# The last 64 rows of the contraction in an mLSTM and bilinear kernel: half-array pairs of matmuls against full-array matmuls on a stacked tile

## The chip, the cores and the metric

The kernel runs on one core of a Trainium2 chip. The metric is the device time of one execution in microseconds. A core has a tensor engine (PE; its weight loads are listed apart as PEld), a vector engine (DVE), a scalar engine (ACT), GpSimd (POOL) and a queue engine (SP) that issues all DMAs of this kernel in the order in which they stand on it.

## The reference

```python
# per batch b and head h, over 768 steps t (B=4, H=8, D=40)
m_new = maximum(f[t] + m, i[t])
C = exp(f[t] + m - m_new) * C + exp(i[t] - m_new) * outer(v[t], k[t])
n = exp(f[t] + m - m_new) * n + exp(i[t] - m_new) * k[t]
y[t] = sigmoid(o[t]) * (C @ q[t]) / maximum(abs(n . q[t]), 1)
# then over all 3072 tokens, x = y with its 8 heads of 40 side by side: 320 columns
a = x @ w_a              # 320 x 1536
b = x @ w_b              # 320 x 1536
out = (a * b) @ w_out    # 1536 x 320
```

The weights come as float64. The bilinear layer contracts over 320 rows of x: two full tiles of 128 rows and a last one of 64. That last one is what the change is about.

## The kernel before

**Attention.** The 768 steps of each of the four sequences are cut into chunks of 128 tokens, 24 chunks in all, and `chunks` lists them by step and sequence. A chunk goes through stages named by letters: decay weights (E), splits and transposes of q and k (A), scores (B), values (C), the denominator and the gated output y (F), the state's update (U), and last `stage_d`, which turns y to x. y lies in the tile `osig`, tokens on the partitions and 320 columns in the free dimension. `stage_d` transposes it into one PSUM tile `pX` of 3 x 128 columns and evicts it in two parts: a rounded high part (`xh`, float32r) and the rest (`xl`).

**The last 64 columns of y.** `stage_d` writes them twice: a transpose puts them into rows 0 to 63 of the third part of pX (L596), and an ordinary matmul with the identity puts the same columns into rows 64 to 127 (L597). Rows 0 to 63 of `xh[:, 2]` become the high part. For rows 64 to 127 ACT copies the high part into a tile of its own, `xd` (L602), and DVE writes the low part into `xh[64:, 2]` (L606). The third part of xh so holds high above low.

**Bilinear layer.** The chunks are grouped into nine token blocks of `sizes = [2, 2, 3, 3, 3, 3, 3, 2, 3]` chunks, so a matmul of the layer streams 256 or 384 columns. `moe_block` walks over the 12 hidden tiles `ff` of 128 columns. For each, `up` accumulates w_a's product in `acc[0]` and w_b's in `acc[1]` (PSUM tiles `pu`, three buffers). An exact product is built from three terms (high times high, high times low, low times high) for each of the first two row tiles: six matmuls on the full 128 x 128 array (L694). For the last 64 rows a seventh one takes `wh[j][:, 2]`, in which the high part of the weights stands in both halves, times `xh[:, 2]`. The low weights of these rows are in a tile `wt`, those of w_a in rows 0 to 63 and those of w_b in rows 64 to 127, and two matmuls of 64 rows (L702) multiply them: `wt[0:64]` times `xh[0:64, 2]` into acc[0], and `wt[64:]` times `xd[64:]` into acc[1]. ACT (or DVE) copies acc[0] to `g`, DVE multiplies acc[1] by it, splits the product, and `down` (L664) multiplies it by w_out into `pd`, two hidden tiles later.

**Weights.** `weights` turns the float64 words into float32r parts in 32 stages, eight for each group of 384 columns, spread over roughly the first 135 us. The fifth stage of a group is that of the last 64 rows: ACT rounds the high parts (L338), two DMAs on SP's queue copy each of them into the other half of `wh[j][:, 2]` (L341), and the low parts go to `wt`, by POOL in the first two groups and by PE and an ACT copy in the last two (L360).

**Order.** Pieces of attention are mixed into the matmuls of a token block at a fixed rate (the last loop of the program), and a scheduler then sets the order on each engine before the kernel runs; on the chip each engine follows that order.

Of the kernel before, what the change touches and what calls it, by code (L numbers as in the profile page):

```python
# [20 lines left out]
def kernel(  # L21
# [37 lines left out]
    wh = [wpool.tile([P, 3, DFF], F32R, name=f"wh{j}") for j in range(2)]  # L59
    wl = [wpool.tile([P, 2, DFF], F32R, name=f"wl{j}") for j in range(2)]  # L60
    wt = wpool.tile([P, DFF], F32R, name="wt")
# [11 lines left out]
    # words on their way to the weights, in the room of q's and k's parts till then  # L73
# [8 lines left out]
    # constants and parts of the first chunks' exponents, in the last state's room till then  # L82
# [14 lines left out]
    # columns of log inputs, state weights and the next chunk's decays, chunk by chunk  # L97
# [8 lines left out]
    sizes = [2, 2, 3, 3, 3, 3, 3, 2, 3]       # chunks of a token block  # L106
# [41 lines left out]
    def load_o(c):  # L148
        """Output gates of a chunk of every sequence."""
        osig[c] = apool.tile([P, B, DM], F32, tag="osig", name=f"osig{c}", bufs=1)  # L150
        for b in range(B):
            nc.sync.dma_start(
                osig[c][:, b].rearrange("t (h d) -> t h d", h=H),
                o_gate[b, :, c * P:(c + 1) * P, :].rearrange("h t d -> t h d"),
            )
        hot[0] = 3
        nc.scalar.activation(osig[c], osig[c], AF.Sigmoid)
# [22 lines left out]
        # the first chunks' log decays and inputs, and their parts as bfloat16  # L180
# [21 lines left out]
        # the later chunks  # L202
# [51 lines left out]
    def weight_stages():  # L254
        for ch in range(DFF // WCH):
            cols = slice(ch * WCH, (ch + 1) * WCH)
            for kt in range(2):
                for j, w in ((0, w_a), (1, w_b)):
# [11 lines left out]
                cols,  # L270
# [9 lines left out]
    def need(x):  # L280
        """Weight stages before x are emitted."""
        while ready[0] < x:
            next(conv)

    def weights():
# [46 lines left out]
        def second(x):  # L332
# [3 lines left out]
            kept = [(rows, h, l) for rows, h, l in hl if l is not None]  # L336
            for rows, h, l in kept:
                nc.scalar.copy(h, W[rows])  # L338
            if len(hl) == 4:
                for j in range(2):  # L340
                    nc.sync.dma_start(  # L341
                        hl[j * 3 + (1 - 2 * j)][1].bitcast(F32), hl[3 * j][1].bitcast(F32)
                    )
            if x < 2 * STAGES and x % STAGES < 6 or x < 2 * STAGES:
                for rows, h, l in kept:
                    nc.gpsimd.tensor_tensor(W[rows], W[rows], h.bitcast(F32), op=ALU.subtract)
                (nc.gpsimd if x < 2 * STAGES and x % STAGES < 6 else nc.vector).tensor_tensor(low(x), W, r, op=ALU.add)
                return
            pc = ps_up.tile([P, NTB], F32, tag="pu", name=f"pc{x}")[:, :n]
            if x % STAGES < (4 if x < 2 * STAGES else STAGES):  # L350
                for rows, h, l in kept:
                    nc.gpsimd.tensor_tensor(l, W[rows], h.bitcast(F32), op=ALU.subtract)
                nc.tensor.matmul(pc, eye[0], low(x), start=True, stop=False)
                nc.tensor.matmul(pc, eye[0], r, start=False, stop=True)
            else:
                nc.tensor.matmul(pc, ident, W, start=True, stop=False)
                nc.tensor.matmul(pc, eye[0], r, start=False, stop=False)
                for rows, h, l in kept:
                    nc.tensor.matmul(pc[rows], eye[1][rows, rows], h, start=False, stop=True)
            nc.scalar.copy(low(x), pc)  # L360
# [21 lines left out]
    def stage_e(n):  # L382
        """Decay weights of a chunk, masked to s <= t."""
# [14 lines left out]
    def stage_a(n):  # L398
        """Exact three-part bfloat16 splits of q, k and v; q and k transposed on the way."""
# [6 lines left out]
        # parts of a head's row: q as (h, h, m) and (h, m, l), k as (m, h, h) and (l, m, h)  # L406
# [152 lines left out]
    def stage_f(n):  # L559
# [14 lines left out]
        yv = y.rearrange("p (h d) -> p h d", h=H)  # L574
# [7 lines left out]
    def stage_d(n):  # L582
# [3 lines left out]
        if t0 == 0:  # L586
            xt[k_] = (
                mpool.tile([P, 3, NTB], F32R, tag="xh", name=f"xh{k_}", bufs=2),
                mpool.tile([P, 2, NTB], F32R, tag="xl", name=f"xl{k_}", bufs=2),
                mpool.tile([P, NTB], F32R, tag="xd", name=f"xd{k_}", bufs=2),  # L590
            )
        xh, xl, xd = xt[k_]
        pX = ps_at.tile([P, 512], F32, tag="pat", name=f"pX{n}")
        for t in range(2):
# [346 lines left out]
```

## Time and profile before

| what | value |
|---|---|
| time, median of 3 runs | 642.67 us (635.86 to 645.09) |
| span of the profiled execution, first to last instruction | 641.1 us |
| PE busy (matmuls) | 604.1 us, 94%, 4926 matmuls |
| DVE busy | 478.1 us, 75% |
| ACT busy | 240.8 us, 38% |
| POOL busy | 206.5 us, 32% |
| mean granted clock of the tensor engine | 0.944 |

The profile gives no other time of its own execution than its span, which is 1.6 us below the median of the timed runs. A matmul's duration in the trace covers its whole way through the array, and matmuls overlap; what one costs is the distance from its start to the start of the next. A row of the timeline has the start and the duration in us, the engine, the line, the operation, what it writes and reads, and the tile. Rows that follow each other with the same text are merged (x2).

### The profile page before, as it was taken

The numbers are of one execution on the slowest core, as the hardware profiler recorded it, in microseconds if no ns is written. First come the engines' busy times: TensorE is split into PE (matmuls) and PEld (weight loads), VectorE is DVE, ScalarE is ACT, GpSimd is POOL, SyncE is SP. The second block draws the span as 40 slices with busy tenths as digits, with TensorE's granted clock in tenths as the row PEclk, the third lists the DMA queues.
The fourth block names the chain that finished last, engine by engine and source line by source line (L and its number), as shares of the span: only waits on it lengthen the run. The fifth ranks groups of instructions, "written<-read, shape, count | busy, mean of one in ns | idle before, by whom it ended". The sixth has DMA issues, their size and how long they took to land. (4 is left out here: it accounts for less than half of the span.)

```text
span 641.1 us, 12928 instructions
## 1 busy us (share of the span) xinstructions
PE 604.1 (94%) x4926; PEld 525.6 (82%) x4926; DVE 478.1 (75%) x1012; ACT 240.8 (38%) x562; POOL 206.5 (32%) x230
## 2 busy tenths in 40 slices
PE   4766998999999999999999999989999999999997
PEld 3554887888878888888888888878898899888896
DVE  6999899875785979689686889589949674843332
ACT  5645456564332353233433244343414512310011
POOL 2778665654440343044213233213303301100000
PEclk9655988698999999999999999989999999999999
DMA  9565656464445486347943645637635903300000
GB/s 195 97 164 129 149 131 155 140 133 89 118 101 85 107 153 147 77 122 138 172 83 97 136 100 117 162 88 117 137 83 121 170 11 91 52 1 22 0 1 32
DMA packets 196339, 67.66 MB, mean 106 GB/s; under 512 B 178452, under 2 KB 189556, under 8 KB 196276
## 3 DMA queue, kind: packets, MB, share of 16 engines
q1 hardware_dynamic: 196276, 66.83, 48.2%
q8 instruction: 39, 0.64, 0.4%
q14 instruction: 24, 0.20, 0.1%
HBM read 41.18 MB, written 5.97 MB: 74 GB/s over the span
## 5 line engine op out<-in xcount | busy, mean ns | idle before, releaser
L694 PE MATMUL pu<-xh,wh 128*128 128x384 f32 (+1 forms) x648 | 219.3, 344 | 1.3 <-ACT xh L601 1.3
L694 PE MATMUL pu<-xl,wh 128*128 128x384 f32 (+1 forms) x432 | 142.1, 329 | 0.4 <-DVE xl L603 0.4
L694 PE MATMUL pu<-xh,wl 128*128 128x384 f32 (+1 forms) x432 | 141.0, 326 | 0.0
L694 PEld LDWEIGHTS pu<-xh,wh 128*128 128x128 f32 x648 | 124.6, 194 | 19.9 <-issue 13.6
L709 DVE TENSOR_TENSOR g<-pu,g 128x384 f32<-128x384 f32 (+1 forms) x108 | 55.0, 509 | 97.6 <-PE pu L694 57.3
L708 ACT COPY g<-pu 128x384 f32<-128x384 f32 (+1 forms) x90 | 39.7, 442 | 141.9 <-PE pu L702 129.1
L664 PE MATMUL pd<-woh,gh 128*128 128x320 f32 x288 | 92.4, 323 | 0.0
L664 PE MATMUL pd<-wol,gh 128*128 128x320 f32 x288 | 89.6, 313 | 0.0
L664 PE MATMUL pd<-woh,gl 128*128 128x320 f32 x288 | 86.4, 316 | 0.0
L694 PEld LDWEIGHTS pu<-xl,wh 128*128 128x128 f32 x432 | 84.0, 194 | 1.7 <-DVE xl L603 0.6
L694 PEld LDWEIGHTS pu<-xh,wl 128*128 128x128 f32 x432 | 83.8, 194 | 0.7 <-issue 0.7
L491 POOL TENSOR_TENSOR vw<-va,gtab 128x336 f32<-128x336 f32 x14 | 11.3, 805 | 175.5 <-PE pU L525 153.3
L664 PEld LDWEIGHTS pd<-woh,gh 128*128 128x128 f32 x288 | 54.8, 190 | 4.4 <-issue 2.9
L394 ACT ACTIVATE gbc<-gbc,gtab 128x128 f32<-128x128 f32 x160 | 49.1, 389 | 16.6 <-POOL gbc L387 16.4
L664 PEld LDWEIGHTS pd<-wol,gh 128*128 128x128 f32 x288 | 54.9, 190 | 0.5 <-issue 0.5
L664 PEld LDWEIGHTS pd<-woh,gl 128*128 128x128 f32 x288 | 53.4, 190 | 0.5 <-issue 0.3
L713 DVE TENSOR_TENSOR gl<-g,gh 128x384 fp32r<-128x384 f32 (+1 forms) x92 | 50.7, 551 | 1.8
L711 DVE CAST gh<-g 128x384 fp32r<-128x384 f32 (+1 forms) x108 | 45.8, 424 | 1.7
L702 PE MATMUL pu<-xh,wt 64*128 64x384 f32 (+1 forms) x108 | 46.2, 428 | 0.0
L702 PE MATMUL pu<-xd,wt 64*128 64x384 f32 (+1 forms) x108 | 46.2, 427 | 0.0
L575 POOL TENSOR_TENSOR osig<-osig,den 128x320 f32<-128x320 f32 x24 | 19.5, 814 | 68.4 <-DVE den L570 50.7
L387 POOL TENSOR_SCALAR_AFFINE_SELECT gbc<-gbc 128x1024 f32<-128x1024 f32 x20 | 25.6, 1279 | 43.0 <-DMA va<-in_v_dram 32.4
(153 smaller groups left out, 1173.8 us busy)
## 6 DMA issues: line engine op xcount, KB each, us to landing
gbc<-g_dram SPq DMA_DIRECT2D x20, 512.0 KB
va<-in_v_dram SPq DMA_DIRECT2D x24, 160.0 KB
qk<-in_q_dram SPq DMA_DIRECT2D x24, 160.0 KB
qk<-in_k_dram SPq DMA_DIRECT2D x24, 160.0 KB
osig<-in_o_gate_dram SPq DMA_DIRECT2D x24, 160.0 KB
raw<-in_moe_w_out_dram SPq DMA_DIRECT2D x12, 320.0 KB
out_dram<-o SPq DMA_DIRECT2D x24, 160.0 KB
raw<-in_moe_w_a_dram SPq DMA_DIRECT2D x8, 384.0 KB
```

What stands on the lines that cost most here:

```text
L387: nc.gpsimd.affine_select(E, E, pattern=[[0, H], [1, P]], compare_op=ALU.is_ge, fill=-1e30, base=0, channel_multiplier=-1,)
L394: nc.scalar.activation(E[:, h], E[:, h], AF.Exp, bias=beta[:, h:h + 1])
L491: nc.gpsimd.tensor_tensor(vw, nat(n)[1], w_col(c, b).unsqueeze(2).broadcast_to([P, H, DV]), op=ALU.mult)
L575: after["p"] = [nc.gpsimd.tensor_tensor(yv, yv, den.unsqueeze(2).broadcast_to([P, H, D]), op=ALU.mult).ins]
L664: nc.tensor.matmul(pd[t][:, 0:DM], a[:, cols], w[:, ff, :], start=(ff == 0 and first), stop=(ff == NF - 1 and last),)
L694: nc.tensor.matmul(acc[j], a, r, start=(j == 0 and x == 0), stop=(j == 1 and x == len(terms) - 1),)
L702: nc.tensor.matmul(acc[h], wt[h * 64:h * 64 + 64, cols], r, start=(h == 1), stop=(h == 0))
L708: (nc.vector.tensor_copy if ff in [1, 2] else nc.scalar.copy)(g, acc[0])
L709: nc.vector.tensor_tensor(g, acc[1], g, op=ALU.mult)
L711: nc.vector.tensor_copy(gh, g)
L713: (nc.gpsimd if kb * 12 + ff < 16 else nc.vector).tensor_tensor(gl, g, gh.bitcast(F32), op=ALU.subtract)
```

## The change

The last 64 rows no longer use half-array matmuls.

- y gets 64 more columns: `osig` is 384 wide for each sequence, and after DVE has written y, ACT copies its last 64 columns behind it (one new instruction for each chunk, in `stage_f`).
- `stage_d` makes three full 128 x 128 transposes. The third yields the last 64 columns in both halves. One ACT copy writes xh and one DVE subtraction writes xl, both 3 x 128 wide. The tile `xd`, its ACT copy and the second DVE subtraction are gone.
- The weights of the last 64 rows are stacked: `wh[0][:, 2]` holds w_a's high part in rows 0 to 63 and its low part in rows 64 to 127, `wh[1][:, 2]` the other way round. The low parts are made in a staging tile `ct` with one buffer and reach their half by two DMAs on SP's queue, issued after the low parts are made (before, the DMAs carried the high parts and were issued after those). `wt` is gone.
- In `up` each accumulator takes eight full-array matmuls: the stacked tile times `xh[:, 2]` and times `xl[:, 2]` in place of the seventh matmul and the pair. The count stays 16 for each hidden tile.

```diff
     def load_o(c):
-        osig[c] = apool.tile([P, B, DM], F32, tag="osig", name=f"osig{c}", bufs=1)
+        osig[c] = apool.tile([P, B, 3 * P], F32, tag="osig", name=f"osig{c}", bufs=1)
...
                 [
-                    (slice(j * 64, j * 64 + 64), wh[j][u * 64:u * 64 + 64, 2, cols],
-                     wt[j * 64:j * 64 + 64, cols] if u == j else None)
-                    for j in range(2) for u in range(2)
+                    (slice(j * 64, j * 64 + 64), wh[j][j * 64:j * 64 + 64, 2, cols],
+                     wh[j][64 - j * 64:128 - j * 64, 2, cols])
+                    for j in range(2)
                 ],
...
         def low(x):
-            hl = stages[x][1]
-            return hl[0][2] if len(hl) == 1 else wt[:, stages[x][2]]
+            hl = stages[x][1]
+            if len(hl) == 1:
+                return hl[0][2]
+            return cpool.tile([P, WCH], F32R, tag="ct", name="ct", bufs=1)
+
+        def cross(x, lo):
+            hl = stages[x][1]
+            if len(hl) > 1:
+                for rows, h, l in hl:
+                    nc.sync.dma_start(l.bitcast(F32), lo[rows].bitcast(F32))
...
-            if len(hl) == 4:
-                for j in range(2):
-                    nc.sync.dma_start(
-                        hl[j * 3 + (1 - 2 * j)][1].bitcast(F32), hl[3 * j][1].bitcast(F32)
-                    )
...
-            nc.scalar.copy(low(x), pc)
+            nc.scalar.copy(lo, pc)
+            cross(x, lo)
...
         nc.vector.tensor_tensor(yv, num[:, :, 0:D], yv, op=ALU.mult)
+        nc.scalar.copy(y[:, DM:], y[:, 2 * P:DM])
...
-        for t in range(2):
+        for t in range(3):
             nc.tensor.transpose(pX[:, t * P:(t + 1) * P], s["y"][:, t * P:(t + 1) * P], ident)
-        nc.tensor.transpose(pX[0:64, 2 * P:3 * P], s["y"][:, 2 * P:], ident)
-        nc.tensor.matmul(pX[64:, 2 * P:3 * P], s["y"][:, 2 * P:], ident, start=True, stop=True)
...
         after["a"] = [nc.scalar.copy(xh[:, :, cols], px).ins]
-        nc.scalar.copy(xd[64:, cols], px[64:, 2])
         nc.vector.tensor_tensor(
-            xl[:, :, cols], px[:, 0:2], xh[:, 0:2, cols].bitcast(F32), op=ALU.subtract
-        )
-        nc.vector.tensor_tensor(
-            xh[64:, 2, cols], px[64:, 2], xd[64:, cols].bitcast(F32), op=ALU.subtract
+            xl[:, :, cols], px, xh[:, :, cols].bitcast(F32), op=ALU.subtract
         )
...
-                    (wh[j][:, 2, cols], xh[:, 2, :]),
+                    (wh[j][:, 2, cols], xh[:, 2, :]), (wh[j][:, 2, cols], xl[:, 2, :]),
                 ]
                 for x, (a, r) in enumerate(terms):
                     nc.tensor.matmul(
-                        acc[j], a, r, start=(j == 0 and x == 0),
-                        stop=(j == 1 and x == len(terms) - 1),
+                        acc[j], a, r, start=(x == 0), stop=(x == len(terms) - 1),
                     )
                     yield
-                if j == 0:
-                    for h, r in enumerate((xh[0:64, 2, :], xd[64:, :])):
-                        nc.tensor.matmul(
-                            acc[h], wt[h * 64:h * 64 + 64, cols], r, start=(h == 1), stop=(h == 0)
-                        )
-                        yield
```

The scheduler sets the order anew. On PE, in hidden tile 8 of the eighth token block (two chunks), this stood before around the two half-array matmuls (`pu_8_0` is acc[0], `pu_8_1` is acc[1], wh_72 and wh_73 are w_a's and w_b's high parts, pd is the output of `down`):

```order
L694 MATMUL pu_8_0_7524<-xl_6400,wh_72 128x256
L694 MATMUL pu_8_0_7524<-xh_6399,wl_74 128x256
L694 MATMUL pu_8_0_7524<-xh_6399,wh_72 128x256
L702 MATMUL pu_8_0_7524<-xh_6399,wt 128x256
L664 MATMUL pd_0_6921<-woh,gh_6_7483 128x320
L664 MATMUL pd_0_6921<-wol,gh_6_7483 128x320
L702 MATMUL pu_8_1_7525<-xd_6401,wt 128x256
L694 MATMUL pu_8_1_7525<-xh_6399,wh_73 128x256
L694 MATMUL pu_8_1_7525<-xl_6400,wh_73 128x256
```

And at the same place now:

```order
L693 MATMUL pu_8_0_7470<-xl_6359,wh_72 128x256
L693 MATMUL pu_8_0_7470<-xh_6358,wl_74 128x256
L693 MATMUL pu_8_0_7470<-xh_6358,wh_72 128x256
L693 MATMUL pu_8_0_7470<-xl_6359,wh_72 128x256
L662 MATMUL pd_0_6874<-woh,gh_6_7429 128x320
L662 MATMUL pd_0_6874<-wol,gh_6_7429 128x320
L693 MATMUL pu_8_1_7471<-xh_6358,wh_73 128x256
L693 MATMUL pu_8_1_7471<-xl_6359,wh_73 128x256
```

The two half-array matmuls, here apart with two matmuls of `down` between them, are gone; the eighth term of acc[0] stands in the place of the first. In the whole order before, 85 of the 108 pairs stand next to each other and 23 are apart; of the 36 pairs of two-chunk blocks 20 are together and 16 apart, of the 72 of three-chunk blocks 65 and 7.

On PE, `stage_d` of a chunk in the middle of the program stood before like this (pX is its PSUM tile, osig the tile of y, and a row with x2 is two instructions):

```order
L595 MATMUL pX_4734<-ident,osig_3792 128x128 x2
L596 MATMUL pX_4734<-ident,osig_3792 64x128
L597 MATMUL pX_4734<-ident,osig_3792 64x128
L694 MATMUL pu_7_0_5014<-xh_3543,wl_74 128x384
L694 MATMUL pu_7_0_5014<-xh_3543,wh_72 128x384
L702 MATMUL pu_7_0_5014<-xh_3543,wt 128x384
L702 MATMUL pu_7_1_5015<-xd_3545,wt 128x384
```

Now it is:

```order
L599 MATMUL pX_4704<-ident,osig_3766 128x128 x3
L693 MATMUL pu_7_0_4979<-xh_3523,wl_74 128x384
L693 MATMUL pu_7_0_4979<-xh_3523,wh_72 128x384
L693 MATMUL pu_7_0_4979<-xl_3524,wh_72 128x384
L693 MATMUL pu_7_1_4980<-xh_3523,wh_73 128x384
```

The two 64-row outputs became one of 128 rows, and the neighbours are the same.

On SP's queue, the two DMAs that fill the other half of `wh[j][:, 2]` for the second group of weight columns stood before in this stretch (cb and c_dram carry a state of the attention to DRAM, cx brings it back, raw are float64 weights):

```order
L551 DMA c_dram_120<-cb_843 40x336
L341 DMA wh_72<-wh_72 64x384
L164 DMA gbc_641<-g_dram 128x1024
L296 DMA raw<-in_moe_w_out_dram 128x320
L341 DMA wh_73<-wh_73 64x384
L134 DMA qk_88<-in_q_dram 128x8x40
L134 DMA qk_88<-in_k_dram 128x8x40
L296 DMA raw<-in_moe_w_a_dram 128x384
```

Now they stand here:

```order
L555 DMA c_dram_119<-cb_839 40x3x336
L294 DMA raw<-in_moe_w_b_dram 128x384
L557 DMA cx_0_99<-c_dram_119 120x336
L294 DMA raw<-in_moe_w_a_dram 128x384
L557 DMA cx_1_100<-c_dram_119 120x336
L309 DMA wh_72<-ct 64x384
L309 DMA wh_73<-ct 64x384
L554 DMA c_dram_120<-cb_1172 40x336
```

They moved from ahead of the state's large write (L552 before, L555 now) to behind both of the reads of it (L554 before, L557 now), which wait for that write to land.

More of the change, by code (lines that the diff above doesn't have):

```diff
@@ L148, in load_o @@
     def load_o(c):
-        osig[c] = apool.tile([P, B, DM], F32, tag="osig", name=f"osig{c}", bufs=1)
+        osig[c] = apool.tile([P, B, 3 * P], F32, tag="osig", name=f"osig{c}", bufs=1)
         for b in range(B):
             nc.sync.dma_start(
-                osig[c][:, b].rearrange("t (h d) -> t h d", h=H),
+                osig[c][:, b, 0:DM].rearrange("t (h d) -> t h d", h=H),
                 o_gate[b, :, c * P:(c + 1) * P, :].rearrange("h t d -> t h d"),
@@ L156, in load_o @@
         hot[0] = 3
-        nc.scalar.activation(osig[c], osig[c], AF.Sigmoid)
+        nc.scalar.activation(osig[c][:, :, 0:DM], osig[c][:, :, 0:DM], AF.Sigmoid)
     def load_g(n):
@@ L335, in second @@
             hl = stages[x][1]
-            kept = [(rows, h, l) for rows, h, l in hl if l is not None]
-            for rows, h, l in kept:
+            lo = low(x)
+            for rows, h, _ in hl:
                 nc.scalar.copy(h, W[rows])
-            if len(hl) == 4:
-                for j in range(2):
-                    nc.sync.dma_start(
-                        hl[j * 3 + (1 - 2 * j)][1].bitcast(F32), hl[3 * j][1].bitcast(F32)
-                    )
             if x < 2 * STAGES and x % STAGES < 6 or x < 2 * STAGES:
-                for rows, h, l in kept:
+                for rows, h, _ in hl:
                     nc.gpsimd.tensor_tensor(W[rows], W[rows], h.bitcast(F32), op=ALU.subtract)
-                (nc.gpsimd if x < 2 * STAGES and x % STAGES < 6 else nc.vector).tensor_tensor(low(x), W, r, op=ALU.add)
+                (nc.gpsimd if x < 2 * STAGES and x % STAGES < 6 else nc.vector).tensor_tensor(lo, W, r, op=ALU.add)
+                cross(x, lo)
                 return
@@ L350, in second @@
             if x % STAGES < (4 if x < 2 * STAGES else STAGES):
-                for rows, h, l in kept:
-                    nc.gpsimd.tensor_tensor(l, W[rows], h.bitcast(F32), op=ALU.subtract)
-                nc.tensor.matmul(pc, eye[0], low(x), start=True, stop=False)
+                for rows, h, _ in hl:
+                    nc.gpsimd.tensor_tensor(lo[rows], W[rows], h.bitcast(F32), op=ALU.subtract)
+                nc.tensor.matmul(pc, eye[0], lo, start=True, stop=False)
                 nc.tensor.matmul(pc, eye[0], r, start=False, stop=True)
@@ L357, in second @@
                 nc.tensor.matmul(pc, eye[0], r, start=False, stop=False)
-                for rows, h, l in kept:
+                for rows, h, _ in hl:
                     nc.tensor.matmul(pc[rows], eye[1][rows, rows], h, start=False, stop=True)
-            nc.scalar.copy(low(x), pc)
+            nc.scalar.copy(lo, pc)
+            cross(x, lo)
         fetch(0)
@@ L573, in stage_f @@
         y = osig[c][:, b]
-        yv = y.rearrange("p (h d) -> p h d", h=H)
+        yv = y[:, 0:DM].rearrange("p (h d) -> p h d", h=H)
         after["p"] = [nc.gpsimd.tensor_tensor(yv, yv, den.unsqueeze(2).broadcast_to([P, H, D]), op=ALU.mult).ins]
         nc.vector.tensor_tensor(yv, num[:, :, 0:D], yv, op=ALU.mult)
+        nc.scalar.copy(y[:, DM:], y[:, 2 * P:DM])
         s["y"] = y
@@ L588, in stage_d @@
                 mpool.tile([P, 3, NTB], F32R, tag="xh", name=f"xh{k_}", bufs=2),
-                mpool.tile([P, 2, NTB], F32R, tag="xl", name=f"xl{k_}", bufs=2),
-                mpool.tile([P, NTB], F32R, tag="xd", name=f"xd{k_}", bufs=2),
+                mpool.tile([P, 3, NTB], F32R, tag="xl", name=f"xl{k_}", bufs=2),
             )
-        xh, xl, xd = xt[k_]
+        xh, xl = xt[k_]
         pX = ps_at.tile([P, 512], F32, tag="pat", name=f"pX{n}")
-        for t in range(2):
+        for t in range(3):
             nc.tensor.transpose(pX[:, t * P:(t + 1) * P], s["y"][:, t * P:(t + 1) * P], ident)
-        nc.tensor.transpose(pX[0:64, 2 * P:3 * P], s["y"][:, 2 * P:], ident)
-        nc.tensor.matmul(pX[64:, 2 * P:3 * P], s["y"][:, 2 * P:], ident, start=True, stop=True)
         yield
@@ L651, in moe_block @@
         NT = sizes[kb] * P
-        xh, xl, xd = (x[..., 0:NT] for x in xt.pop(kb))
+        xh, xl = (x[..., 0:NT] for x in xt.pop(kb))
         pd = [ps_dn.tile([P, 512], F32, tag=f"pd{t}", name=f"pd{kb}_{t}") for t in range(sizes[kb])]
```

2 lines of the change are left out of this document (removed).

## The prediction

> **What bounds the kernel now.** I read the page first, then the chain that ended last, then the busy time by stage. These are lines of the page and of the table of stages (stretch, length, then busy us of PE, PEld, DVE, ACT, POOL with the number of instructions, the granted clock, the DMA share and GB/s):
>
> ```profile
> span 641.1 us, 12928 instructions
> PE 37%; DVE 1%; issue 1%; ACTq 0%; ACT 0%; DVEq 0%
> 60.00:120.00 60.00, 57.22 (x370) 48.33 (x369) 55.33 (x108) 32.17 (x74) 38.89 (x39) 0.85 0.60 151
> 120.00:641.00 521.00, 510.78 (x4324) 448.36 (x4322) 369.11 (x816) 178.06 (x429) 130.24 (x143) 0.99 0.45 96
> 360.00:400.00 40.00, 39.40 (x378) 34.80 (x378) 35.63 (x78) 14.48 (x37) 13.87 (x14) 1.00 0.54 119
> ```
>
> From 120 us on PE is busy for 510.78 of 521 us at nearly full clock, and the chain, which can be followed back over some two fifths of the span, is PE almost alone. A shorter interval between two PE instructions is worth its own length there. From 60 to 120 us DVE (55.33 of 60) is as full as PE, since it converts the weights; a gain of PE counts for little.
>
> **The half-array pair, three-chunk block.** The timeline of PE around one pair, and then the same in a two-chunk block:
>
> ```profile
> 302.38 0.34 PE L694 MATMUL pu<-xh,wh 128*128 128x384 f32 x1
> 302.65 0.44 PE L702 MATMUL pu<-xh,wt 64*128 64x384 f32 x1
> 302.65 0.44 PE L702 MATMUL pu<-xd,wt 64*128 64x384 f32 x1
> 303.02 0.44 PE L694 MATMUL pu<-xh,wh 128*128 128x384 f32 x1
> 303.30 0.34 PE L694 MATMUL pu<-xl,wh 128*128 128x384 f32 x1
> 303.47 0.34 PE L694 MATMUL pu<-xh,wl 128*128 128x384 f32 x1
> ...
> 560.20 0.28 PE L694 MATMUL pu<-xh,wh 128*128 128x256 f32 x1
> 560.41 0.38 PE L702 MATMUL pu<-xh,wt 64*128 64x256 f32 x1
> 560.42 0.38 PE L702 MATMUL pu<-xd,wt 64*128 64x256 f32 x1
> 560.73 0.39 PE L694 MATMUL pu<-xh,wh 128*128 128x256 f32 x1
> 560.95 0.28 PE L694 MATMUL pu<-xl,wh 128*128 128x256 f32 x1
> 561.07 0.27 PE L694 MATMUL pu<-xh,wl 128*128 128x256 f32 x1
> ```
>
> Look at starts. Two full matmuls follow each other after 0.17 us (303.30 to 303.47). The two halves do start together, so two matmuls pass in the time of one. But the step into the pair takes 0.27 (302.38 to 302.65), the pair 0.37, and the first full matmul after it 0.28 (303.02 to 303.30): 0.92 us from 302.38 to 303.30. After the change four full matmuls stand there, 4 x 0.175 = 0.70 (0.175 lies between the 0.17 read here and the 0.18 that other such rows round to). Saved: **0.22 us**. In the two-chunk block 560.20 to 560.95 is 0.75, and four full ones are 4 x 0.12 = 0.48: **0.27 us**. So changing between full and half array costs about 0.1 us each way, and the pair itself is no faster than two full matmuls.
>
> The Trainium skill has both sides of this in "TensorEngine Tiling (Array Packing)". Section Overview (Theoretical Speedup) gives up to twice the speed for a dimension of 64 or less, which speaks against the change; section Tiling Modes (Key Properties) says that changing the tiling mode drains the engine. By the first alone a pair would cost one slot. The trace agrees that the halves run at once, and shows by the row of 302.38 to 303.30 that the changes of mode eat it.
>
> **Pairs that stand apart.** In 23 of the 108 hidden tiles the scheduler had put other work between the halves:
>
> ```profile
> 567.62 0.28 PE L694 MATMUL pu<-xh,wh 128*128 128x256 f32 x1
> 567.83 0.38 PE L702 MATMUL pu<-xh,wt 64*128 64x256 f32 x1
> 568.13 0.41 PE L664 MATMUL pd<-woh,gh 128*128 128x320 f32 x1
> 568.39 0.31 PE L664 MATMUL pd<-wol,gh 128*128 128x320 f32 x1
> 568.62 0.38 PE L702 MATMUL pu<-xd,wt 64*128 64x256 f32 x1
> 568.94 0.39 PE L694 MATMUL pu<-xh,wh 128*128 128x256 f32 x1
> 569.16 0.28 PE L694 MATMUL pu<-xl,wh 128*128 128x256 f32 x1
> ```
>
> 567.62 to 569.16 is 1.54 us. With full matmuls it is four of 0.12 and two of `down` at 0.15 (the next view shows 221.80 to 221.95): 0.78. Saved: **0.76 us**. For three chunks I put each half at 0.37 plus two changes at 0.1, 0.57, against 0.175 for a full one: 2 x 0.395 = **0.79 us**.
>
> Sum over the order before: 65 x 0.22 + 20 x 0.27 + 16 x 0.76 + 7 x 0.79 = 14.3 + 5.4 + 12.2 + 5.5 = **37.4 us** of PE time. The order after has none of the 216 left.
>
> **The transposes.** One chunk on PE:
>
> ```profile
> 220.73 0.42 PE L595 MATMUL pX<-ident,osig 128*128 128x128 f32 x2
> 220.98 0.27 PE L596 MATMUL pX<-ident,osig 128*64 128x128 f32 x1
> 221.19 0.43 PE L597 MATMUL pX<-ident,osig 128*64 128x128 f32 x2
> 221.55 0.42 PE L664 MATMUL pd<-woh,gl 128*128 128x320 f32 x1
> 221.80 0.31 PE L664 MATMUL pd<-woh,gh 128*128 128x320 f32 x1
> 221.95 0.31 PE L664 MATMUL pd<-wol,gh 128*128 128x320 f32 x1
> ```
>
> The two full transposes take 0.25 together (220.73 to 220.98). L596 takes 0.21, L597 (one matmul in the program, two passes in the trace) 0.36, and the first matmul behind them 0.25 instead of 0.15: 0.67 beyond what is needed without them. A third full transpose costs about 0.11, which I read as less than half of the two, the first having a start-up. Saved: **0.56 us** for each of 24 chunks, **13.4 us**.
>
> **How much of it lies where PE sets the time.** These are the rows from 120 us on for L702, then for L597, in a table of stages of that line alone (here only PE and PEld busy stand ahead of the clock):
>
> ```profile
> 120.00:641.00 521.00, 50.63 (x200) 22.32 (x200) 0.99 0.45 96
> 120.00:641.00 521.00, 9.48 (x42) 4.11 (x42) 0.99 0.45 96
> ```
>
> 200 of 216 halves and 42 of 48 passes: 37.4 x 200/216 + 13.4 x 42/48 = 34.6 + 11.7 = **46.3 us**. Ahead of 120 us some 4.5 us of PE time go, of which I count none by itself.
>
> **DVE and ACT.** Mean durations of their groups (line, engine, operation, names, shapes, count, busy us, mean ns):
>
> ```profile
> L603 DVE TENSOR_TENSOR xl<-pX,xh 128x256 fp32r<-128x256 f32 x24 | 9.9, 414 | 0.6 <-ACT xd L602 0.5
> L606 DVE TENSOR_TENSOR xh<-pX,xd 64x128 fp32r<-64x128 f32 x24 | 7.1, 295 | 0.3
> L709 DVE TENSOR_TENSOR g<-pu,g 128x384 f32<-128x384 f32 x72 | 39.9, 554 | 72.1 <-PE pu L694 39.0 <-ACT g L708 32.5
> L602 ACT CAST xd<-pX 64x128 fp32r<-64x128 f32 x24 | 6.3, 261 | 0.4
> ```
>
> DVE: 414 + 295 leave, one subtraction of 384 columns comes, 554 by L709, which reads PSUM at that width: 24 x 155 ns = 3.7 us less of DVE. ACT: 261 ns leave (L602) and a copy of 128 x 64 comes, not in this trace. I take L602's 261, the nearest row in size, with nothing and the 554 of the wide operation of L709 as its ends. ACT is busy for 178 of 521 us, so that is nothing by itself. Its place matters more (a rival below).
>
> With 46 us less from 120 us on, DVE's 369 us lie in 475: 78%. In the densest stage, 360 to 400, PE saves about 3.6 us (46.3 over thirteen such stages), and DVE's 35.63 us then fill 98% of 36.4. So some waits for DVE come out that PE's length hid. From nothing to half of the gain can be lost; I take a tenth, **4.6 us**, since the other stages are far emptier.
>
> **The two DMAs of the low weights.** Before they carried high parts and were early; now they wait for the low parts, and on SP they stand behind the reads of the state:
>
> ```profile
> 27.82 0.34 SPq L238 DMA_DIRECT2D dec<-e_dram  x1
> 31.23 0.31 ACT L239 ACTIVATE dec<-dec 128x128 f32<-128x128 f32 x1 [0.40 <-DMA dec<-e_dram]
> 77.27 0.80 SPq L554 DMA_DIRECT2D cx<-c_dram  x2
> 80.60 0.28 PE L694 MATMUL pu<-xh,wh 128*128 128x256 f32 x1
> ```
>
> The DMA of dec took 3.4 us from issue to its reader, which waited for it. In the second group the reads of the state were issued until 78.1; the two DMAs behind them then land at about 81.5 to 83, and the first matmul that needs them ran at 80.60: PE stands for **1 to 3 us**, and everything behind it. In the third and fourth groups the low parts come out of PE by an ACT copy shortly before they are needed; the 3.4 us of the DMA are between covered by other PE work and nearly bare: 0 to 3 us each. Sum 1 to 9, I take 4.5, as much as PE saves ahead of 120 us: the two cancel. The first group is covered: its readers come 20 us later.
>
> **The sum.** 641.1 - 46.3 + 4.6 - 4.5 + 4.5 = 599.4 us of span. The median of the timed runs is 1.6 above the span shown: **601 us**.
>
> **Rivals.**
> - *DVE takes over* (0.17). PE's gaps behind DVE grow until half of the gain is back: 642.7 - 23 = 620. For it: 35.63 of 40 in one stage. Against it: 369 of 521 in the mean, and DVE's own wait of 39 us for L694 shows that PE is ahead of it in the chain.
> - *The pair is worth one slot after all* (0.09): the 0.1 us steps are not a cost of changing modes but belong to the change of accumulator, which stays. Then each pair is replaced by two slots: + 72 x 0.175 + 36 x 0.12 = 16.9, less 13.4 for the transposes: 646. The plain theoretical speed-up that the Trainium skill names in "TensorEngine Tiling (Array Packing)", section Overview, would come out like this. The trace speaks against it with 302.65 to 303.02 for a pair and 0.17 for a full one.
> - *ACT's queue stalls* (0.04), the case that ends slower. The new copy waits in ACT's fixed order for DVE's y, and what stands behind it (the exponentials, the bf16 casts, the evictions of acc[0]) waits too. Each us that this takes uncovered, in each of 24 chunks, costs 24 us; from 42 / 24 = 1.75 us per chunk the gain is gone, at 2.5 the time is 661. For it: the copy stands right ahead of those in several chunks. Against it: ACT is idle for two thirds of the span.
> - That the change does not remove the halves is excluded by the order shown.
>
> **How the numbers follow.** Forecast 0.70 (590 to 612), DVE 0.17 (612 to 628), one slot 0.09 (640 to 652), ACT 0.04 (above 656). The range 588 to 626 takes in the first two down to their ends and leaves out about 0.15. Beyond 2%, about what a measurement can tell from no change, faster begins below 630: 0.87; same 0.09; slower 0.04.
>
> **What would show it.** Right: from 120 us on the eight matmuls of an accumulator follow at 0.175 or 0.12 us without a step; a chunk's pX rows take 0.36 us; PE keeps 95% or more of its span. A PE gap of 1 to 3 us before the first `up` of a weight group, released by a DMA on wh, confirms the fourth term. Wrong: PE gaps behind DVE's gh or gbc in the middle of the program (DVE takes over), steps of 0.1 us that stay where the halves were (one slot), or ACT's new copy idle for over 1 us behind osig with DVE and PE waiting on ACT (ACT's queue).

## The result and the profile after

The changed kernel takes **619.58 us** (median of 4 runs, 618.15 to 620.73) against 643.88 us (median of 4 runs, 635.86 to 647.91): a ratio of **0.9643, 95% interval 0.9572 to 0.9714**. That is 24 us less, where 42 were forecast. The time lies in the range on record, 588 to 626, because that range takes in the rival *DVE takes over* (612 to 628); the forecast's own stretch, 590 to 612, missed it, and 619.6 is nearly that rival's 620. (The ratios here and below leave out the runs that a slower state of the chip disturbed, the medians do not, so they can differ by a few tenths of a per cent.)

The page of the changed kernel: its span, its busy times and the chain that ended last:

```profile
span 617.3 us, 12778 instructions
PE 561.1 (91%) x4878; PEld 529.1 (86%) x4878; DVE 480.4 (78%) x988; ACT 235.9 (38%) x562; POOL 207.1 (34%) x230
PE 23%; DVE 2%; DMA 1%; SPq 1%; issue 1%; ACT 0%; ACTq 0%
```

PE's share of its span fell from 94% to 91%: the work became shorter, and idle time appeared. The chain points the same way, though it can now be followed back over only some 28% of the span, where it was two fifths: PE had 37% of the span in it before, and DVE and issue 1% each; now PE has 23%, with 2% of DVE and 1% each of DMA and SP's queue between. The table of stages shows it best (stretch, length, then busy us of PE, PEld, DVE, ACT, POOL):

```profile
120.00:617.00 497.00, 470.53 (x4256) 452.85 (x4255) 372.18 (x795) 171.53 (x421) 129.81 (x143) 0.99 0.47 101
```

Idle of PE from 120 us on: 26.5 us, against 521 - 510.78 = 10.2 before.

**What the change does on PE is as it was read.** Timeline of the changed kernel, one accumulator of three chunks, one of two, and a chunk's transposes:

```profile
295.26 0.34 PE L693 MATMUL pu<-xh,wl 128*128 128x384 f32 x1
295.44 0.33 PE L693 MATMUL pu<-xh,wh 128*128 128x384 f32 x1
295.61 0.33 PE L693 MATMUL pu<-xl,wh 128*128 128x384 f32 x1
295.79 0.33 PE L693 MATMUL pu<-xh,wl 128*128 128x384 f32 x1
...
545.18 0.28 PE L693 MATMUL pu<-xh,wl 128*128 128x256 f32 x1
545.30 0.28 PE L693 MATMUL pu<-xh,wh 128*128 128x256 f32 x1
545.42 0.28 PE L693 MATMUL pu<-xl,wh 128*128 128x256 f32 x1
...
299.16 0.55 PE L599 MATMUL pX<-ident,osig 128*128 128x128 f32 x3 [0.28 <-DVE gbc L457]
299.46 0.42 PE L693 MATMUL pu<-xh,wl 128*128 128x384 f32 x1
```

The starts follow at 0.17 to 0.18 and at 0.12 us with no step left. The three transposes take 0.30 (299.16 to 299.46); 0.36 was foretold.

**Where it was lost: PE's waits.** The view of waits, PE alone, from 154 us on (who waits, for what, us in total, times, longest). First before, whole, then after:

```profile
PE pX L595 <- DVE gbc L454: 3.9, 4, 1.7
PE pI L475 <- DVE gbc L454: 1.8, 2, 1.5
```

```profile
PE pI L478 <- DVE gbc L457: 7.6, 8, 2.2
PE pX L599 <- DVE gbc L457: 5.8, 6, 2.0
PE pS L452 <- DMA T<-qks: 2.9, 2, 2.3
PE pu L693 <- ACT g L699: 2.2, 4, 1.0
PE pd L662 <- POOL gl L704: 1.2, 1, 1.2
PE pV L504 <- DVE pb L463: 0.9, 1, 0.9
```

pI (the product with the state carried from the chunk before) and pX take slots of a ring of two PSUM buffers (`ps_at`), which the scores pS hold until DVE has multiplied them into the decay weights gbc. PE now gets there before DVE has.

**The sum of PE's intervals.** From the starts of PE's rows I took, for each kind of matmul (output, columns), its usual distance to the next start. What exceeds it by over 0.4 us in one place is counted as a wait, the rest is PE's own pace. The first token block ends when ACT has copied its last output; the stretch goes from there to the last matmul. In us, each from one profiled execution (e1 to e12 are the experiments below):

| kernel | first block ends | stretch | PE's own pace | waits |
|---|---|---|---|---|
| before | 151.9 | 484.3 | 477.0 | 7.3 |
| after | 153.6 | 459.4 | 435.7 | 23.7 |
| e1, pairs at full rows | 155.5 | 461.1 | 449.0 | 12.1 |
| e2, old transposes | 165.6 | 458.0 | 444.2 | 13.8 |
| e3, copy on DVE | 158.9 | 454.3 | 434.5 | 19.8 |
| e4, after without gl | 152.5 | 446.9 | 433.8 | 13.1 |
| e8, DMAs early | 148.8 | 461.5 | 439.9 | 21.6 |
| e9, before without gl | 151.9 | 479.9 | 475.4 | 4.5 |
| e10, some of gl on POOL | 154.9 | 461.6 | 438.6 | 23.0 |
| e11, denser mixing | 156.1 | 454.7 | 436.4 | 18.3 |
| e12, pX in up's ring | 155.5 | 510.8 | 455.3 | 55.5 |

PE's own pace gained **41.3 us**, the waits gave back **16.4**, and the first block (0 to 151.9 before, 0 to 153.6 after) 1.7: 23.2, where the spans differ by 23.8.

The table shows more than the sum. From before to e1, PE's own pace falls by 28.0 us and the waits rise by 4.8. From e1 to after it falls by another 13.3, and the waits rise by 11.6; from e2 to after it falls by 8.5, and they rise by 9.9. So most of the first part of the cut was kept, and nearly all of the last part came back as waits.

By token blocks, the first being block 0 (us from the last output of the block before to its own last):

| block (chunks) | 1 (2) | 2 (3) | 3 (3) | 4 (3) | 5 (3) | 6 (3) | 7 (2) | 8 (3) |
|---|---|---|---|---|---|---|---|---|
| before | 54.6 | 65.8 | 67.9 | 66.9 | 69.3 | 60.5 | 49.9 | 50.7 |
| after | 45.6 | 65.4 | 68.5 | 64.4 | 64.9 | 61.9 | 42.9 | 46.9 |
| waits before | 1.9 | 0.6 | 1.6 | 0.8 | 2.4 | 0 | 0 | 0 |
| waits after | 4.0 | 3.8 | 5.7 | 1.2 | 4.8 | 4.2 | 0 | 0 |

Blocks 7 and 8, in which PE waits for nothing, keep what they gained, 7.0 and 3.8 us, and block 1, into which the program's last loop mixes fewer pieces of attention than into those behind it, 9.0. The five blocks of three chunks with the full share of attention, 330.4 us together before, are 325.1 now: 5.3 us of gain, with 14.3 us of new waits.

**One such wait, on three engines.** Timeline of the changed kernel, first PE, then DVE, then ACT:

```profile
316.72 0.34 PE L693 MATMUL pu<-xh,wh 128*128 128x384 f32 x1
319.11 0.56 PE L478 MATMUL pI<-cx,T 120*128 120x42 bf16 x16 [2.06 <-DVE gbc L457]
...
294.50 0.48 DVE L579 TENSOR_TENSOR osig<-num,osig 128x320 f32<-128x320 f32 x1
313.35 0.56 DVE L700 TENSOR_TENSOR g<-pu,g 128x384 f32<-128x384 f32 x1 [6.13 <-ACT g L699]
313.83 2.45 DVE L579 TENSOR_TENSOR osig<-num,osig 128x320 f32<-128x320 f32 x1
318.39 1.27 DVE L457 TENSOR_TENSOR gbc<-pS,gbc 128x512 f32<-128x512 f32 x2
...
310.02 1.28 ACT L156 ACT_TABLE_LOAD   x1 [8.75 <-DMA osig<-in_o_gate_dram]
```

PE stands 2.06 us for DVE's gbc. But DVE itself had stood still for 6.13 us until 313.35, for ACT's copy of acc[0], and ACT had stood 8.75 us at the sigmoid, for the load of the output gates. DVE then needed 2.45 us for the multiplication that makes y (L579), which took 0.48 one chunk earlier (the row of 294.50); POOL was at work from 312.67 to 315.93 beside it (the last section has more of this). So the engine named by the wait was late in a chain, and on top of that was slow in one of its links, by about as much as PE waited. L579 has such long cases in the kernel before too (up to 2.86 us), so the change did not make them.

### The profile page after: what moved, and what is told of

Same layout as the page of the kernel before. It is cut to its first block, busy times and chain, and to the rows that moved or that the text cites. A ratio compares the mean times of both kernels' runs of the same rounds, so it can differ in the third digit from the quotient of the medians.

```text
span 617.3 us, 12778 instructions
## 1 busy us (share of the span) xinstructions
PE 561.1 (91%) x4878; PEld 529.1 (86%) x4878; DVE 480.4 (78%) x988; ACT 235.9 (38%) x562; POOL 207.1 (34%) x230
## 5 line engine op out<-in xcount | busy, mean ns | idle before, releaser
L693 PE MATMUL pu<-xh,wh 128*128 128x384 f32 (+1 forms) x648 | 211.9, 329 | 4.7 <-ACT g L699 2.4
L693 PE MATMUL pu<-xl,wh 128*128 128x384 f32 (+1 forms) x648 | 210.2, 326 | 0.0
L693 PEld LDWEIGHTS pu<-xl,wh 128*128 128x128 f32 x648 | 124.1, 192 | 0.4
L700 DVE TENSOR_TENSOR g<-pu,g 128x384 f32<-128x384 f32 (+1 forms) x108 | 54.6, 506 | 85.1 <-ACT g L699 42.9
L662 PE MATMUL pd<-woh,gh 128*128 128x320 f32 x288 | 88.9, 311 | 0.2 <-DVE gh L702 0.2
L662 PE MATMUL pd<-woh,gl 128*128 128x320 f32 x288 | 85.0, 312 | 1.4 <-POOL gl L704 1.4
L494 POOL TENSOR_TENSOR vw<-va,gtab 128x336 f32<-128x336 f32 x14 | 11.2, 802 | 155.6 <-PE pU L528 155.6
L702 DVE CAST gh<-g 128x384 fp32r<-128x384 f32 (+1 forms) x108 | 51.0, 472 | 1.8
L415 ACT CAST qks<-qk 128x320 bf16<-128x320 f32 x36 | 16.4, 454 | 68.0 <-DMA T<-qks 54.4
L578 POOL TENSOR_TENSOR osig<-osig,den 128x320 f32<-128x320 f32 x24 | 19.7, 821 | 65.4 <-DVE den L573 41.5
L390 POOL TENSOR_SCALAR_AFFINE_SELECT gbc<-gbc 128x1024 f32<-128x1024 f32 x20 | 22.9, 1143 | 43.5 <-DMA gbc<-g_dram 43.1
L459 ACT CAST pb<-gbc 128x512 bf16<-128x512 f32 x36 | 21.7, 618 | 20.2 <-DVE gbc L457 20.2
```

The costliest lines, as they stand in the source:

```text
L390: nc.gpsimd.affine_select(E, E, pattern=[[0, H], [1, P]], compare_op=ALU.is_ge, fill=-1e30, base=0, channel_multiplier=-1,)
L415: nc.scalar.copy(ph, src[:, j])
L459: nc.scalar.copy(pb[:, 0], E)
L494: nc.gpsimd.tensor_tensor(vw, nat(n)[1], w_col(c, b).unsqueeze(2).broadcast_to([P, H, DV]), op=ALU.mult)
L662: nc.tensor.matmul(pd[t][:, 0:DM], a[:, cols], w[:, ff, :], start=(ff == 0 and first), stop=(ff == NF - 1 and last),)
L693: nc.tensor.matmul(acc[j], a, r, start=(x == 0), stop=(x == len(terms) - 1),)
```

## The experiments

Each edit was made alone, on the kernel named. The scheduler sets the order anew for each, so a run differs from its base by more than its edit.

**e1, the pairs alone.** Before, with all 128 rows for both matmuls of the pair (the products are then not those of the last 64 rows; their sizes are what counts):

```diff
-                    for h, r in enumerate((xh[0:64, 2, :], xd[64:, :])):
+                    for h, r in enumerate((xh[:, 2, :], xh[:, 2, :])):
...
-                            acc[h], wt[h * 64:h * 64 + 64, cols], r, start=(h == 1), stop=(h == 0)
+                            acc[h], wt[:, cols], r, start=(h == 1), stop=(h == 0)
```

> The kernel before with one edit: the two 64-row matmuls of a hidden tile read all 128 rows of wt and of xh's third part, so they are full-array matmuls of the same number and the sums of the last 64 rows come out different; transposes, weights and DMAs stay as before. Changes of array mode cost the time (theory): the steps of 0.1 us go, PE has 34.6 us less to do from 120 us on, and if the same half as in the whole change is kept, the time falls by about 18 us, to 625 (0.97). All of it kept: 609 (0.945). Rival, a pair is worth one slot: 17 us slower, 660 (1.026). Rival, the change gained by its transposes and copies alone: no difference, 643.

Measured: 623.01 us, ratio 0.9699 (0.9625 to 0.9773). The edit only makes the two matmuls larger, and 19 us went. The rival "a pair is worth one slot" falls: by it this edit would have cost time. A pair that stands apart in this kernel:

```profile
560.86 0.28 PE L694 MATMUL pu<-xh,wh 128*128 128x256 f32 x1
560.98 0.28 PE L702 MATMUL pu<-xh,wt 128*128 128x256 f32 x1
561.10 0.31 PE L664 MATMUL pd<-woh,gh 128*128 128x320 f32 x1
561.25 0.31 PE L664 MATMUL pd<-wol,gh 128*128 128x320 f32 x1
561.40 0.28 PE L702 MATMUL pu<-xh,wt 128*128 128x256 f32 x1
561.51 0.28 PE L694 MATMUL pu<-xh,wh 128*128 128x256 f32 x1
561.63 0.28 PE L694 MATMUL pu<-xl,wh 128*128 128x256 f32 x1
```

0.77 us from 560.86 to 561.63, where the same six steps took 1.54 before. PE's own pace fell by 28.0 us, its waits rose by 4.8.

**e2, all but the transposes.** After, with the two full transposes, the 64-row transpose and the 64-row matmul of before, and no copy of y's last columns:

```diff
-        nc.scalar.copy(y[:, DM:], y[:, 2 * P:DM])
-        for t in range(3):
+        for t in range(2):
...
+        nc.tensor.transpose(pX[0:64, 2 * P:3 * P], s["y"][:, 2 * P:DM], ident)
+        nc.tensor.matmul(pX[64:, 2 * P:3 * P], s["y"][:, 2 * P:DM], ident, start=True, stop=True)
```

> The kernel after with its transposes undone: y stays 320 wide, no copy on ACT, the third part of pX by a 64-row transpose and a 64-row matmul as before; stacked weights and the eight full matmuls stay. If the transposes' 11.7 us of PE time count in full: 619.6 + 12 = 632. If half of it counts: 626. If ACT's new copy, which waits 38.7 us for DVE's y in its fixed order, is what eats the gain (rival), taking it away brings more than the transposes cost: 605 to 617.

Measured: 630.06 us, ratio 0.9821 (0.9763 to 0.988): 10.5 us more than after, near to the 11.7 forecast, but not where they were forecast. The first block of e2 ends 12.0 us later than that of after (table above), and it holds only 11 of the 48 passes of the old transposes, worth some 3 us by the forecast. From its end on e2 takes 1.4 us less than after: PE's own pace is 8.5 us longer, and its waits are 9.9 shorter. So the transposes' saving is seen on PE, but there the time kept nothing of it, and that the whole differs by about the amount forecast is luck. What does fall is the rival, by which taking ACT's copy away would have gained.

e2 and e1 have nearly the same work on PE (444.2 and 449.0), and e2 is 7 us slower, with a first block that ends 10.1 us later. e2 also has the new weights and their late DMAs; but after has them too, and its first block ends at 153.6. A difference of some us in the first block between two builds proves no cause by itself.

**e3, the copy of y on DVE instead of ACT.** `nc.scalar.copy` of L581 became `nc.vector.tensor_copy`.

> The kernel after with the copy of y's last 64 columns on DVE, right behind the multiplication that makes y, instead of on ACT. Rival (ACT's queue stalls behind the copy): ACT's 38.7 us of waits for y go, the evictions and exponentials behind it come earlier, 605 to 612. Theory (DVE's queue is what PE waits for): DVE has about 24 x 0.2 = 5 us more, the time stays or grows a little, 619 to 623.

Measured: 620.76 us, ratio 0.9673 (0.9601 to 0.9745), as after. The copy's wait for y on ACT is large in after, second row below, and taking it off ACT brought nothing clear of noise; the rival "ACT's queue stalls" falls. (Waits of ACT in after; L156 is the sigmoid.)

```profile
ACT L156 <- DMA osig<-in_o_gate_dram: 21.3, 4, 8.8
ACT osig L581 <- DVE osig L579: 38.7, 18, 4.3
```

**e4 and e9, is DVE too full?** The product g of acc[0] and acc[1] is split into a rounded part gh and the rest gl. After and before, each without DVE's 92 subtractions that make gl. The third matmul of `down` reads gh in its place, so the low part of the product is missing in the output:

```diff
-            (nc.gpsimd if kb * 12 + ff < 16 else nc.vector).tensor_tensor(
-                gl, g, gh.bitcast(F32), op=ALU.subtract
-            )
+            if kb * 12 + ff < 16:
+                nc.gpsimd.tensor_tensor(gl, g, gh.bitcast(F32), op=ALU.subtract)
+            else:
+                gl = gh
```

> The kernel after without DVE's 92 subtractions that make gl (50.0 us of DVE); the third matmul of down reads gh in its place, so the out values lack the low part of the product from hidden tile 16 on; PE's work is the same. Theory (DVE's queue gives back the gain): PE's waits behind DVE's gbc and osig shrink, the time falls by 12 to 20 us, to 600 to 608. Rival (the new order or ACT's queue costs it, not DVE's load): under 5 us, 615 to 620.

> The kernel before, with the same 92 subtractions of gl left out of DVE as in e4 (the third matmul of down reads gh instead, so the product's low part is not computed); it is the control for e4, which went from 619.6 to 611.5 us. Theory A (the change shortens PE until DVE's load shows, so DVE is a bound only after it): before, PE waits over 0.4 us were 7.8 us in all from 130 us on, so leaving out 50 us of DVE work gives at most 3 us: 638 to 643, ratio 0.995 to 1.00. Theory B (the subtractions cost the same in both, by the work they put into g, gh, gl ahead of down, and have nothing to do with the change): 8 us less as in e4, 633 to 635, ratio 0.987. If B, the 8 us of e4 are no part of what the change gave back.

Measured: e4 611.5 us, ratio 0.9548 (0.9475 to 0.9621); e9 637.88 us, ratio 0.9902 (0.987 to 0.9934). e4 alone looks like the rival "DVE takes over" come true: 50 us of DVE work less, 8.1 us gained. The control says otherwise. In the kernel before, where PE hardly waited, the same cut gains 6.2 us (between the ranges of the two theories), and in ratios the two are equal: 0.9548 / 0.9643 = 0.990, and 0.990. So these subtractions cost time in both kernels, and by the times the change did not make them dearer. The profiled executions say something else: the cut takes 10.6 us off the waits in after (23.7 to 13.1), and 2.8 in before (7.3 to 4.5); but e4's was the fastest of its four runs, 604.96 us. With intervals of 0.7% either way on e4 and on after, some 6 us are not excluded.

**e5, gh on ACT for all blocks but the first.** `nc.vector.tensor_copy(gh, g)` became `nc.scalar.copy(gh, g)` there.

> The kernel after with the rounding of the product, gh, on ACT instead of DVE from the second token block on (96 of 108 casts, about 45 us off DVE and onto ACT, which is busy for 236 us). Theory (DVE's load gives back the gain): like the run without gl, 608 to 613. Rival (it is not DVE's load but the wait for PSUM or for DMAs; or ACT, now longer in the chain of g, becomes the bound): 618 to 630.

Measured: 625.31 us, ratio 0.9819 (0.9716 to 0.9922): slower than after. The waits of e5 have new rows:

```profile
ACT gh L702 <- DVE g L700: 93.1, 77, 3.5
DVE gl L704 <- ACT gh L702: 36.2, 47, 6.9
```

g, gh and gl are one chain, and it now changes its engine twice more. DVE lost work and won waits.

**e6, output gates in six tiles of one sequence.** The load of a step's gates waits for fewer readers, and four sigmoids stand in the place of one:

```diff
-        osig[c] = apool.tile([P, B, 3 * P], F32, tag="osig", name=f"osig{c}", bufs=1)
+        osig[c] = [
+            apool.tile([P, 3 * P], F32, tag="osig", name=f"osig{c}_{b}", bufs=6) for b in range(B)
+        ]
...
-        nc.scalar.activation(osig[c][:, :, 0:DM], osig[c][:, :, 0:DM], AF.Sigmoid)
+        for y in osig[c]:
+            nc.scalar.activation(y[:, 0:DM], y[:, 0:DM], AF.Sigmoid)
```

> The kernel after with the output gates in six tiles of one sequence each, not one tile for four, so that the DMAs of the next step's gates need not wait for the last transposes of y; four sigmoids of 320 columns in place of one of 1280. Theory (a part of the loss is ACT standing for those DMAs, 21.3 us in 4 waits, with the evictions of acc[0] behind it): the waits shrink, 610 to 616. Rival (ACT's wait is hidden, only DVE's load counts): 618 to 622.

Measured: 628.29 us, ratio 0.9801 (0.9703 to 0.9898): a miss. ACT's wait for the gates is not shorter in sum (27.4 us in 13 waits, where after has 21.3 in 4), and the first block grew by 11 us. Whether an earlier load would help stays open.

**e7 and e12, other slots for pI and pX.** The waits are for slots of the ring of two, so e7 takes both out of it (pX from the seventh chunk on) into the ring of up's accumulators, which has three, and e12 pX alone:

```diff
-            pI = ps_at.tile([P, 512], F32, tag="pat", name=f"pI{n}")
+            pI = ps_up.tile([P, NTB], F32, tag="pu", name=f"pI{n}")
...
-        pX = ps_at.tile([P, 512], F32, tag="pat", name=f"pX{n}")
+        pX = ps_up.tile([P, NTB], F32, tag="pu", name=f"pX{n}") if n > 5 else ps_at.tile(
+            [P, 512], F32, tag="pat", name=f"pX{n}")
```

> The kernel after with pI and (from the seventh chunk on) pX in the PSUM ring of up (three buffers) instead of that of the attention (two buffers), so that neither waits until DVE has read the two halves of pS. Theory (PE's visible waits are for those two buffers, 13.4 us behind DVE's gbc): they go, 608 to 614. Rival (PE is ahead of DVE in any case, and only waits elsewhere, or up's ring becomes short): 617 to 630.

> The changed kernel with pX alone (the transposes' output, from the seventh chunk on) in the ring of up's accumulators (three buffers) instead of the ring of two of the attention; pI stays, unlike e7. Theory A (PE's waits for pI and pX, 13 us in the rows of the changed kernel, come of the ring of two): pX no longer waits for gbc and the ring serves the others sooner, 3 to 6 us faster, 614 to 617. Theory B (as e7's 43 us showed, up's ring has no slot to spare): a third of e7's loss, 10 to 20 us slower, 630 to 640.

Measured: e7 662.46 us, ratio 1.0373 (1.0292 to 1.0454); e12 671.08 us, ratio 1.0435 (1.039 to 1.048). Both lose everything and more, e7 more than either theory gave, and e12 not a third of e7's loss as expected but at least as much. The waits of PE in e12 from 154 us on, the three largest rows:

```profile
PE pX L600 <- DVE osig L579: 16.1, 9, 4.0
PE pV L504 <- DVE pb L463: 7.2, 7, 3.3
PE pS L452 <- DMA T<-qks: 5.4, 4, 2.4
```

The wait for a slot turned into a wait for y itself, at a larger price, and new waits came in the other stages of the chunk. Whether e12 is worse than e7 is open, as their intervals overlap; why both lose so much was not settled.

**e8, the two DMAs early again.** After, with the DMAs carrying high parts as soon as these are there; the low parts of the last 64 rows go unused.

```diff
-            if len(hl) > 1:
-                for rows, h, l in hl:
-                    nc.sync.dma_start(l.bitcast(F32), lo[rows].bitcast(F32))
+            return
...
+            if len(hl) > 1:
+                for rows, h, l in hl:
+                    nc.sync.dma_start(l.bitcast(F32), h.bitcast(F32))
```

> The kernel after with the two DMAs of a weight group carrying the high parts and issued as soon as these are made, as before; the low parts of the last 64 rows are made but not used, so out lacks them. Theory of the prediction (the late DMAs cost 1 to 9 us in the first token block): 611 to 618, and the first block ends 1 to 9 us earlier. Rival (they are covered): 619 to 621.

Measured: 617.78 us, ratio 0.9666 (0.9606 to 0.9726): by the median 1.8 us less than after, by the ratio nothing, with some 4 us of interval either way. The first block ends 4.8 us earlier than in after, which is what the theory asked for, but 2.1 of that go again behind it, and e3 and after, whose weights are the same, differ by 5.3 in the first block. So the runs do not decide between the two. In after, PE's own wait for the DMAs is small:

```profile
PE pu L693 <- DMA wh<-ct: 0.6, 1, 0.6
```

**e10, a third of the subtractions of gl on POOL** in the five middle blocks (`kb * 12 + ff < 16 or (1 < kb < 7 and ff % 3 == 1)`).

> The changed kernel, with every third subtraction of gl in the five blocks with three chunks and attention moved from DVE to POOL: 20 of the 60 there. DVE loses 20 x 0.54 = 11 us of work where e4 took away 33 us in these blocks and gained 8. Theory A (DVE's amount of work is what holds PE): a third of e4's gain, 2 to 3 us, 616 to 618. Theory B (what counts is the chain of attention across engines, or the time POOL takes from DVE when both run: gl took 0.54 on DVE alone and 0.99 beside POOL): POOL's 20 subtractions of about 1.3 us lengthen DVE's neighbours and the way to down, 620 to 626.

Measured: 623.08 us, ratio 0.9619 (0.9563 to 0.9675): the interval holds after's ratio, and also the 2 to 3 us of theory A, so no theory is told apart by it.

**e11, attention mixed in more densely**, over 85% of a block's matmuls:

```diff
-            acc += units / (total * 0.93)
+            acc += units / (total * 0.85)
```

> The changed kernel with the pieces of attention mixed into a token block's matmuls over 85% of the block instead of 93%; all work is the same, and the order moves on every engine. Theory A (the loss comes from waits in attention's chain, which gets 9% less room in each block): 3 to 8 us slower, 623 to 628. Theory B (the loss comes of attention's late end in a block, whose y the next block needs; an earlier end helps): 3 to 6 us faster, 614 to 617. If the time stays within 2 us the density of the mixing is not what decides.

Measured: **611.0 us, ratio 0.9498 (0.9456 to 0.954)**. This computes all that the reference asks, and is the fastest such kernel here: 8.6 us below after by the median, with an interval that does not touch after's. The direction is that of theory B, the size is above its 3 to 6. Waits of PE from 154 us on, the three largest rows:

```profile
PE pI L478 <- DVE gbc L457: 5.4, 5, 2.1
PE pS L452 <- DMA T<-qks: 3.4, 1, 3.4
PE pX L599 <- DVE gbc L457: 3.3, 6, 0.7
```

Against after, those for gbc fell from 13.4 to 8.7 us, and all waits by the table above from 23.7 to 18.3, at the same pace of PE. This is an indication only: the profiled execution, 617.23 us, is the slowest of the six. So one number that sets where attention lies among the matmuls is worth as much as all of e4's cut. Why 0.85 is better was not settled, and whether it helps the kernel before as well was not tried.

## Why the prediction was partly right

- **The pairs: right in kind.** Half-array pairs cost two changes of mode and gained nothing: e1. From the first block's end on 189 of the 216 halves are left, 37.4 x 189 / 216 = 32.7 us by the forecast; PE's own pace in e1 fell by 28.0. The Trainium skill's "TensorEngine Tiling (Array Packing)", section Tiling Modes (Key Properties), says that a change of mode drains the engine; e1, which takes away the changes of mode and keeps the rest of the program, agrees with its 19 us.
- **The transposes: right on PE, not in the time.** From the first block's end on 40 of the 48 passes are left, 13.4 x 40 / 48 = 11.2 us; PE's own pace fell by 8.5 from e2 to after and by 13.3 from e1 to after. The waits rose by 9.9 and 11.6 with it. The 10.5 us by the medians of e2 and after agree with the forecast by luck, since e2 loses them in its first block.
- **PE's own pace in sum: near.** 46.3 forecast from 120 us on, 32.7 + 11.2 = 43.9 of them from 152 on; 41.3 measured from 152 on.
- **The give-back: the step that failed.** "From nothing to half of the gain can be lost; I take a tenth, 4.6 us". The waits grew by 16.4 us, two fifths of 41.3. The reason given for the small end, "the other stages are far emptier", used busy shares of DVE. The waits came in the chain instead: in the stretch shown PE waited for DVE, DVE for ACT, ACT for the load of the gates, and DVE was slow beside POOL. The signs on record agree: PE was to keep 95% of its span and kept 91%, and the gaps behind gbc, named as a sign of *DVE takes over*, came.
- **The DMAs of the low weights: not settled.** 4.5 us (1 to 9) forecast, with a gap of 1 to 3 us on PE as the sign; PE waits for them for 0.6 us. In e8 the first block ends 4.8 us earlier, but the time is 1.8 us less by the medians and no less by the ratios. In the first block the 4.5 were to cancel with 4.5 gained on PE; it lost 1.7, although the granted clock over the first 152 us was 0.88 in after and 0.80 in before.
- **The sum.** 5.0 less from PE (2.4 of them because the measured stretch begins later), 11.8 more in waits, 1.7 in the first block: 18.5, which takes 601 to 619.5, where 619.6 was measured.
- **The rivals.** *DVE takes over* gave the right number, 620, and the waits are indeed behind gbc. Its reason, that DVE is too full, is not shown: the times of e4 and e9 speak against it, their profiles in part for it. *One slot* is refuted by e1, *ACT's queue* by e3. DVE's saving came as foretold in its own rows (xl is now one subtraction of 549 ns instead of 414 + 295), though DVE in sum was busy 480.4 us, 2.3 more than before; ACT's copy takes 244 ns where 261 were taken:

```profile
L604 DVE TENSOR_TENSOR xl<-pX,xh 128x384 fp32r<-128x384 f32 x24 | 13.2, 549 | 2.8 <-ACT xh L603 2.7
L581 ACT COPY osig<-osig 128x64 f32<-128x64 f32 x24 | 5.9, 244 | 38.7 <-DVE osig L579 38.7
```

**What stays open.** The waits that ate the gain stand at pI, pX and pS in blocks 1 to 6. They stay, at 19.8 and 21.6 us, without ACT's new copy (e3) and with the weights' DMAs early (e8), so these two are at most a small part. They respond to how the attention is spread (e11). How far the amount of DVE's work sets them is open: it fell by 50 us in e4 and e9, and their times and their profiles disagree. Which link of that chain is the one to shorten, the runs did not show.

## What to carry to other kernels

Count a half-array matmul by starts, with the step into it and the step out of it, before crediting it with two for one. When the busiest engine is made shorter, part the gain by stages: it stays where that engine works alone, and elsewhere the chains that its length hid come out, at idle shares that look ample, and the later part of a cut can keep far less than the first. After such a cut, try the rate of mixing again (here one number was worth 8.6 us); look at where in the program two runs part before taking their difference for the price of the edit; and where leaving out work on a suspect engine gains time, do the same in the kernel before, or the suspect's old cost is taken for a new one.

## What the runs showed of the hardware

- **Waits of PE go with a lower clock.** In the gappy e12 the granted clock from 200 to 280 us is 0.91, in after 0.98 (the column behind POOL's). The stage of e12, then of after:

```profile
200.00:280.00 80.00, 66.42 (x586) 63.05 (x585) 54.34 (x115) 26.50 (x61) 19.44 (x21) 0.91 0.50 101
```

```profile
200.00:280.00 80.00, 75.21 (x727) 71.50 (x727) 68.39 (x140) 31.20 (x77) 27.15 (x28) 0.98 0.55 120
```

  PE's own pace in e12, which includes waits under 0.4 us, is 19.6 us longer than in after at the same work: a long wait there seems to cost more than its own length. From 154 us to the end the granted clock is 0.95 in e12 and 0.99 in after, which alone would make 454 of the 435.7 us of after's pace (an estimate), and 455.3 were measured. Over whole executions it is 0.89 to 0.93 in all six of e12 and 0.94 to 0.96 in the four of after. This is read from the runs and was not tested by itself.
- **Some of DVE's instructions take much longer beside POOL's.** The same subtraction in after, with POOL's operation at the time of the second:

```profile
287.22 0.54 DVE L704 TENSOR_TENSOR gl<-g,gh 128x384 fp32r<-128x384 f32 x1
292.86 1.07 DVE L704 TENSOR_TENSOR gl<-g,gh 128x384 fp32r<-128x384 f32 x1
...
292.55 0.97 POOL L552 TENSOR_TENSOR cb<-cr,cb 40x336 bf16<-40x336 f32 x1 [0.33 <-POOL gbc L390]
```

  Between 286.51 and 289.07 POOL did nothing, and the subtraction took 0.54; beside POOL's 0.97 it took 1.07. The multiplication L579 takes 0.48 to 0.49 us each time that POOL is idle, and up to 2.86 beside POOL. It is not so for every instruction nor each time: the products that read PSUM (L700, L457) take about the same in both cases, 0.55 and 0.68 us. This is read from the trace and was not tested by itself.
